# Banded attention beside a gated feed-forward layer: the second pass in blocks of 64 keys, its products with v in 64x32 tiles over two PSUM banks, and dense work in two banks

## The chip, the cores and the metric

The kernel runs on one core of one Trainium2 chip. The metric is device microseconds of one execution; the time before is the median of three runs, 883.07 us (882.6 to 883.37).

## The reference, cut to what matters

```python
xn = layernorm(x)                              # x: 2048 tokens x 512
q, k, v = split(xn @ wqkv)                     # 32 heads of 16
scores = q @ k.T * 16**-0.5                    # masked to 0 <= query - key < 256
s = (softmax(scores) @ v).reshape(...) @ wo
g = silu((silu(xn @ w1) * (xn @ w3)) @ w2)     # 512 -> 1792 -> 512
return x + s * g
```

Everything is float32. A query sees itself and the 255 keys before it.

## The kernel before, in words

**Tiling.** The 2048 tokens are cut in NT = 4 stretches t of TW = 512, the 32 heads in NG = 4 groups g of eight, and each group in two halves p of four heads. A unit is (t, g, p); there are 32. Dense products work on float32 numbers split in a high and a low float16 part, three products for one; a dense group is normally 12 matmuls of 128x128 by 512 columns into one PSUM bank: `project` (q or k, L423), `value` (v, L393), `gate_up` (w1 and w3, L684), `down` (w2, L729), `total` (wo, L771). `turn` (L355) transposes x on TensorE for a stretch; `powers` (L203) sums squares of weights in a tiny matmul. All of these, and the transposed maxima `pm` (L492), take their banks from the pool `psm` with three buffers of one bank.

**Attention in two passes.** The first pass (`pass1`) forms scores of 128 queries against up to 320 keys (L476) and takes each row's maximum on VectorE (L481). The maxima, in two float16 parts, become two more rows of q, so that the second pass gets score minus maximum straight from its matmul. The second pass (`pass2`) works with keys on the partitions: `scores(c)` writes a chunk of 128 keys by two blocks of 128 queries, for four heads, into a tile of two banks (L523; `s`, from the pool `pss`, two buffers of two banks, shared with the first pass). The mask is added on VectorE (L532 for a whole chunk, L537 for half of one), then ScalarE's exp (L541) writes `pt` in float32 into SBUF. `values(c)` multiplies `pt` by v (L551) in float32: for each head a tile of 128 rows by 32 columns of the array (16 of v, a column of ones for the sum, and columns that are not used), four heads beside each other, accumulated into `po` (pool `pso`, one bank). `finish` copies `po` out (L559). A unit of t > 0 has six chunks (CHUNKS), one of t = 0 has five (FIRST), the last of them half as wide.

**Order.** TensorE's order is that of the program. `batches` makes the rounds of a unit: in each, two of the second pass's score chunks or the first pass's row blocks (those of the unit two ahead) are emitted; in every second round the products with v that have been kept in `late` follow, and so do the transposed maxima. `spread` puts dense pieces between rounds, by cost. A dense group is two pieces of about six matmuls. The dense pieces of a unit come from two lists, `beside` (projections, v, output products) and the feed-forward's own, and are merged by position, so a group of one list can be half done while groups of the other pass. `later(n, f)` runs f after n more steps (a piece or a round is a step): the readers of a bank are partly emitted this way, one step late. Work marked `urgent` is put ahead on ScalarE's and VectorE's queues. After the last unit what remains of the feed-forward and the last output products run alone.

Of the kernel before, what the change touches and what calls it, by code (L numbers as in the profile page):

```python
# [2 lines left out]

# [17 lines left out]
P = 128  # L21
# [28 lines left out]
VB = 10  # L50
# [14 lines left out]
def tile_block(ctx: ExitStack, tc: tile.TileContext, x, wqkv, wo, w1, w3, w2, out):  # L65
# [18 lines left out]
    psm = pool("psm", 3, PSUM)  # L84
# [18 lines left out]


# [4 lines left out]
    def urgent():  # L109


        return tc.high_priority(offset=200) if started else nullcontext()
# [15 lines left out]
    def flush():  # L128
        while queue:
# [25 lines left out]
    M2 = const.tile([P, 2, P], BF16, name="M2")  # L155
    nc.vector.memset(M2, 0.0)
    nc.gpsimd.affine_select(M2[:, 0, :], M2[:, 0, :], pattern=[[-1, P]], base=0, channel_multiplier=1,
                            compare_op=ALU.is_gt, fill=NEG)
    nc.gpsimd.affine_select(M2[:, 1, :], M2[:, 1, :], pattern=[[1, P]], base=0, channel_multiplier=-1,
                            compare_op=ALU.is_ge, fill=NEG)  # L160
# [36 lines left out]
    def powers(sb, n, p2, inv):  # L197


        ps = psm.tile([P, n], F32, name="ps", tag="mm")  # L200
# [108 lines left out]
    def prepare(t):  # L309
# [32 lines left out]
        def turn(b):  # L342
# [5 lines left out]
            if t or b == 3:  # L348
                pt = psm.tile([P, NC, P], F32, name="mm", tag="mm")
            elif b == 2:  # L350
                pt = pso.tile([P, TW], F32, name="po").rearrange("p (k q) -> p k q", q=P)
            else:
                pt = pss.tile([P, 2, 512], F32, name="s")[:, 0, :].rearrange("p (k q) -> p k q", q=P)
# [25 lines left out]
    def value(j):  # L379
# [18 lines left out]
        return [(6, lambda h=h: part(h)) for h in range(2)]  # L398
# [8 lines left out]
    def project(t, g, k, terms=(range(3),)):  # L407
# [38 lines left out]
        return [(len(l), lambda n=n: part(n)) for n, l in enumerate(parts)]  # L446
# [59 lines left out]
    def pass2(t, g, p):  # L506
# [5 lines left out]

        def scores(c):
            qa, ka = QA[t, g], keys(t, g)
            n = sum(w for _, _, w in chunks[c]) * P
            s = pss.tile([P, 2, 512], F32, name="s")
            for a in range(2):
                o = 256 * a
                for j, q, w in chunks[c]:
                    for k in range(4):  # L520
                        r, h = k % 2, k // 2 * 64
                        rows = slice(64 * r, 64 * r + KR + 2)
                        nc.tensor.matmul(s[h:h + 64, r, o:o + w * P], ka[rows, 2 * p + a, (j + 2) * P + h:(j + 2) * P + h + 64],  # L523
                                         qa[rows, 2 * p + a, q * P:(q + w) * P], start=True, stop=True)
                    o += w * P

            sv = s.rearrange("p r (a b q) -> p (r a) b q", a=2, b=2)
            kinds = [{0: 1, 2: 0}.get(i - j) for j, q, w in chunks[c] for i in range(q, q + w)]
            if None not in kinds and len(kinds) == 2:
                m = M2 if kinds == [0, 1] else M2[:, kinds[0]:kinds[0] + 1, :].to_broadcast([P, 2, P])  # L530
                with urgent():
                    nc.vector.tensor_add(sv, sv, m.unsqueeze(1).to_broadcast([P, 4, 2, P]))  # L532
            else:
                for b, k in enumerate(kinds):
                    if k is not None:
                        with urgent():
                            nc.vector.tensor_add(sv[:, :, b, :], sv[:, :, b, :],  # L537
                                                 M2[:, k:k + 1, :].to_broadcast([P, 4, P]))
            cell[c] = pt = ppool.tile([P, 4, 256], F32, name="pt")
            with urgent():  # L540
                nc.scalar.activation(pt[:, :, 0:n], s.rearrange("p r (a q) -> p (r a) q", a=2)[:, :, 0:n], AF.Exp, scale=es)  # L541

        def values(c):
            if c == 0:
                cell["po"] = pso.tile([P, TW], F32, name="po")
            pt = cell.pop(c)
            o = 0
            for k, (j, q, w) in enumerate(chunks[c]):
                for i in range(4):
                    h = g * 8 + (i // 2) * 4 + 2 * p + i % 2  # L550
                    nc.tensor.matmul(cell["po"][32 * i:32 * i + 32, q * P:(q + w) * P],  # L551
                                     V[:, (4 * t + j) % VB, h * VW:h * VW + 32], pt[:, i, o:o + w * P],
                                     start=c == 0 and k == 0, stop=c == len(chunks) - 1, skip_group_check=True)
                o += w * P

        def finish():
            os = opool.tile([P, TW], F32, name="os")
            with urgent():
                nc.scalar.copy(os, cell["po"])  # L559
# [10 lines left out]
        def last():  # L570
            values(len(chunks) - 1)
            finish()
        n = len(chunks)
        return [lambda c=c: scores(c) for c in range(n)], [lambda c=c: values(c) for c in range(n - 1)] + [last]
# [98 lines left out]
    def gate_up(t, f):  # L673
# [38 lines left out]
        return [lambda k=k, half=half: part(k, half) for k in range(2) for half in range(2)]  # L712
# [368 lines left out]
```

## Time and profile before

| | |
|---|---|
| median of 3 runs | 883.07 us |
| the profiled execution: time, span | 881.5 us, 879.6 us |
| granted TensorE clock | 0.997 |
| busy: TensorE, VectorE, ScalarE, GpSimd | 846.5, 626.7, 443.1, 193.9 us |
| dense matmuls of 512 columns: gate and up (L684), down (L729), projections (L423) | 896 + 448, 672, 384 |
| scores of the second pass (L523), products with v (L551), instructions | 1920, 1920 |
| exp (L541) | 184 of 1093 ns, 200.9 us |

The lines are those of the kernel above. A call of a float32 matmul is two instructions on TensorE. A busy share is no rate: a matmul's duration holds its way through the array, and the next starts before it ends, so prices on TensorE are read from start to start. "Idle before" is the time in which an engine waited, and who ended it.

### The profile page before, as it was taken

What the parts mean: (1) busy time and instruction counts of PE and PEld (TensorE: products, weight loads), DVE (VectorE), ACT (ScalarE), POOL (GpSimd) and SP (SyncE); (2) the same over time, 40 slices, a digit from 0 to 9 for tenths busy, and PEclk for the clock granted to TensorE, in tenths of its full rate; (3) what the DMA queues carried; (4) which work ended last, traced back from release to release, by engine and by line L of the source; (5) the groups of instructions that cost most, each with busy time, mean ns of one, the idle gap of its engine ahead of it and who ended that gap; (6) DMA issues with size and microseconds to landing.
All of it is one profiled execution on the core that took longest, in us unless ns stands there. A gap on an engine that the chain in (4) does not pass through costs nothing.

```text
span 879.6 us, 20432 instructions
## 1 busy us (share of the span) xinstructions
PE 846.5 (96%) x7815; PEld 376.5 (43%) x7815; DVE 626.7 (71%) x1833; ACT 443.1 (50%) x650; POOL 193.9 (22%) x312
## 2 busy tenths in 40 slices
PE   9898898999999999999999999999999999999997
PEld 4333343444444444444444444444444444444443
DVE  8776876877778667787777775776767777666435
ACT  6975877473544444344444445443444444444421
POOL 2254245250201103121110111121111103131211
PEclk9999999999999999999999999999999999999999
DMA  9974534746433353353434344433442253332201
GB/s 293 253 244 148 151 110 126 236 132 222 128 108 70 93 155 107 104 143 98 134 104 103 93 109 135 140 85 104 115 124 84 81 134 115 106 104 82 78 10 59
DMA packets 95073, 110.43 MB, mean 126 GB/s; under 512 B 16960, under 2 KB 60288, under 8 KB 94976
## 3 DMA queue, kind: packets, MB, share of 16 engines
q1 hardware_dynamic: 94688, 108.62, 43.1%
q8 instruction: 61, 1.00, 0.5%
q10 hardware_dynamic: 288, 0.52, 0.2%
q14 instruction: 36, 0.29, 0.1%
HBM read 76.28 MB, written 28.57 MB: 119 GB/s over the span
## 4 chain that ended last, share of the span: by engine, by line
PE 70%; DVE 11%; ACT 5%; issue 4%; DMA 4%; POOL 3%; SPq 2%; POOLq 0%; DVEq 0%; ACTq 0%
PE mm L684 24%; PE mm L729 13%; PE po L551 8%; PE mm L423 6%; PE s L523 6%; PE mm L771 4%; PE s L476 4%; PE mm L393 3%; DVE junk L481 3%; POOL slot L224 2%; DVE s L532 2%; ACT pt L541 1%; DMA slot<-in_A_x_dram 1%; DMA slot<-in_B_w_dram 1%; SPq L590 1%
## 5 line engine op out<-in xcount | busy, mean ns | idle before, releaser
L541 ACT ACTIVATE pt<-s,es 128x1024 f32<-128x1024 f32 (+1 forms) x184 | 200.9, 1093 | 197.5 <-DVE s L532 101.0
L684 PE MATMUL mm<-XH,slot 128*128 128x512 f16 x896 | 268.1, 381 | 0.6 <-POOL slot L224 0.4
L224 POOL TENSOR_TENSOR slot<-slot,slot 128x256 f16<-128x256 f32 (+1 forms) x220 | 146.0, 689 | 529.2 <-ACT slot L708 401.2
L481 DVE CUSTOM_DVE_ANT_0 junk<-s,MW 128x320 bf16<-128x320 f32 x448 | 218.0, 487 | 27.3 <-PE s L476 16.2
L684 PEld LDWEIGHTS <-slot 128*128 128x128 f16 x1344 | 121.6, 98 | 158.9 <-issue 25.2
L684 PE MATMUL mm<-XL,slot 128*128 128x512 f16 x448 | 169.9, 379 | 0.0
L729 PE MATMUL mm<-slot,slot 128*128 128x512 f16 x672 | 160.1, 383 | 0.3
L537 DVE TENSOR_TENSOR s<-s,M 128x512 f32<-128x512 f32 x128 | 89.0, 696 | 62.2 <-PE s L523 53.9
L551 PE MATMUL po<-pt,V 128*32 128x128 f32 (+1 forms) x1920 | 98.3, 330 | 0.0
L729 PEld LDWEIGHTS <-slot 128*128 128x128 f16 x672 | 61.3, 98 | 80.6 <-issue 13.6
L476 PE MATMUL s<-KA,qa 48*64 48x320 f16 (+2 forms) x1024 | 73.6, 298 | 10.7 <-DVE M L481 5.2
L523 PE MATMUL s<-qa,KA 50*64 50x128 f16 (+1 forms) x1920 | 74.2, 251 | 9.9 <-ACT pt L541 6.6
L532 DVE TENSOR_TENSOR s<-s,M 128x1024 f32<-128x1024 f32 x56 | 68.7, 1227 | 15.3 <-PE s L523 13.2
L523 PEld LDWEIGHTS <-KA 50*64 50x64 f16 x1920 | 34.0, 105 | 85.1 <-issue 48.2
L708 ACT CAST slot<-slot 128x512 f16<-128x512 f32 x56 | 34.5, 616 | 61.7 <-DVE slot L704 61.6
L699 DVE SCALAR_TENSOR_TENSOR slot<-slot,mm 128x512 f32<-128x512 f32 x56 | 38.3, 684 | 35.2 <-ACT slot L695 35.1
L551 PEld LDWEIGHTS po<-pt,V 128*32 128x32 f32 x1920 | 49.8, 109 | 24.5 <-issue 11.3
L695 ACT ACTIVATE slot<-mm,sgs 128x512 f32<-128x512 f32 x56 | 38.2, 683 | 31.5 <-PE mm L684 29.8
L224 POOL TENSOR_TENSOR on<-on,rb 128x256 f32<-128x256 f32 x32 | 22.6, 727 | 130.3 <-DMA qa<-dm 50.4
L704 DVE SCALAR_TENSOR_TENSOR slot<-mm,slot 128x512 f32<-128x512 f32 x56 | 38.5, 688 | 17.7 <-PE mm L684 17.6
L745 DVE SCALAR_TENSOR_TENSOR slot<-mm,dsc,slot 128x512 f32<-128x512 f32 x48 | 35.9, 748 | 19.6 <-PE mm L729 19.4
L423 PE MATMUL mm<-XH,whi 128*128 128x512 f16 x128 | 47.2, 381 | 1.3 <-DVE slot L699 0.9
(128 smaller groups left out, 838.3 us busy)
## 6 DMA issues: line engine op xcount, KB each, us to landing
slot<-dW SPq DMA_DIRECT2D x126, 256.0 KB
slot<-in_B_w_dram SPq DMA_DIRECT2D x42, 256.0 KB
dW<-slot SPq DMA_DIRECT2D x42, 256.0 KB
slot<-in_A_x_dram SPq DMA_DIRECT2D x30, 256.0 KB
KA<-dK SPq DMA_DIRECT2D x24, 288.0 KB
qa<-dQ SPq DMA_DIRECT2D x32, 192.0 KB
dK<-slot SPq DMA_DIRECT2D x16, 256.0 KB
dQ<-slot SPq DMA_DIRECT2D x16, 256.0 KB
```

What stands on the lines that cost most here:

```text
L224: op(out[:, c], a[:, c], b[:, c])
L423: nc.tensor.matmul(cell["pp"], a[:, k, c, :], b[:, c, :], start=(c, i) == parts[0][0], stop=(c, i) == parts[-1][-1])
L476: nc.tensor.matmul(s[64 * c:64 * c + 64, r, :n], qa[rows, 2 * p + a, ii * P + 64 * c:ii * P + 64 * c + 64], ka[rows, 2 * p + a, e - n:e], ...
L481: nc.vector.tensor_tensor_reduce(out=junk[:, :n], in0=s[:, r, :n], in1=mask, scale=1.0, scalar=NEG, op0=ALU.add, op1=ALU.max, accum_out=M[ ...
L523: nc.tensor.matmul(s[h:h + 64, r, o:o + w * P], ka[rows, 2 * p + a, (j + 2) * P + h:(j + 2) * P + h + 64], qa[rows, 2 * p + a, q * P:(q + ...
L532: nc.vector.tensor_add(sv, sv, m.unsqueeze(1).to_broadcast([P, 4, 2, P]))
L537: nc.vector.tensor_add(sv[:, :, b, :], sv[:, :, b, :], M2[:, k:k + 1, :].to_broadcast([P, 4, P]))
L541: nc.scalar.activation(pt[:, :, 0:n], s.rearrange("p r (a q) -> p (r a) q", a=2)[:, :, 0:n], AF.Exp, scale=es)
L551: nc.tensor.matmul(cell["po"][32 * i:32 * i + 32, q * P:(q + w) * P], V[:, (4 * t + j) % VB, h * VW:h * VW + 32], pt[:, i, o:o + w * P], s ...
L684: nc.tensor.matmul(cell[k], w[:, (a * NC + c) * P:(a * NC + c + 1) * P], b[:, c, :], start=c == 0 and i == 0, stop=c == NC - 1 and i == 2)
L704: nc.vector.scalar_tensor_tensor(sg, cell[1], 0.5 * HS / (WS * XS)**2, sg, op0=ALU.mult, op1=ALU.mult)
L729: nc.tensor.matmul(ps, hh[:, a * TW + b * P:a * TW + (b + 1) * P], w[:, c * D:(c + 1) * D], start=f == f0 and i == 0, stop=f == f1 - 1 and ...
```

## The change

The second pass takes blocks of 64 keys. Even blocks lie in the lower 64 partitions, odd ones in the upper; a block is scored against the one to five blocks of 64 queries that see it. A piece is (block, first query block after it, how many, slot of 64 columns in the tile, whether v takes it). For t > 0 there are five chunks: two for each of the heads a = 0 and a = 1, and one for both; for t = 0 there are four. A chunk is still one exp of 128x1024. The masks are smaller and applied by slot, in up to two additions to a chunk.

Products with v run in tiles of 64 rows by 32 columns, the lower half of the partitions into the first bank of `po`, the upper half into the second; calls of two chunks alternate. `finish` copies the first bank on ScalarE and adds the second on VectorE. `pso` so has two banks and `psm` two instead of three. To work with two, the two pieces of a dense group are marked (`opening`) and kept next to each other in the list (`in_groups`, `more`); a round can still come between them. `powers` takes its bank from `pss` before the units start. A round with products with v counts 4 instead of 6 (COLS).

```diff
-COLS = 3
-CHUNKS = (((-2, 0, 1), (3, 3, 1)), ((-1, 0, 2),), ((0, 0, 2),), ((0, 2, 1), (1, 3, 1)), ((1, 1, 2),), ((2, 2, 2),))
-FIRST = (((0, 0, 2),), ((0, 2, 1), (1, 3, 1)), ((1, 1, 2),), ((2, 2, 2),), ((3, 3, 1),))
+COLS = 2
+AB = ((0,), (1,))
+CHUNKS = (*((a, ((0, 0, 5, 0, 1), (-2, 2, 3, 5, 1)), ((1, 0, 5, 0, 1), (5, 0, 3, 5, 1)),
+             ((0, 4, 2, 0, 0), (5, 2, 2, 1, 0))) for a in AB),
+          *((a, ((2, 0, 5, 0, 1), (6, 0, 2, 5, 1), (-4, 4, 1, 7, 1)), ((3, 0, 5, 0, 1), (7, 0, 1, 5, 1), (-3, 3, 2, 6, 1)),
+             ((0, 4, 2, 0, 0), (5, 2, 2, 0, 0))) for a in AB),
+          ((0, 1), ((4, 0, 4, 0, 1),), ((-1, 1, 4, 0, 1),), ((0, 3, 2, 2, 0),)))
+FIRST = (*((a, ((0, 0, 5, 0, 1), (6, 0, 2, 5, 1), (4, 3, 1, 7, 1)), ((1, 0, 5, 0, 1), (5, 0, 3, 5, 1)),
+            ((0, 4, 2, 0, 0), (5, 1, 1, 0, 0))) for a in AB),
+         *((a, ((2, 0, 5, 0, 1), (4, 0, 3, 5, 1)), ((3, 0, 5, 0, 1), (7, 0, 1, 5, 1), (3, 1, 2, 6, 0)),
+            ((0, 4, 2, 0, 0), (5, 1, 1, 0, 0))) for a in AB))
...
-    psm = pool("psm", 3, PSUM)
+    psm = pool("psm", 2, PSUM)
...
+    def opening(pieces):
+        for _, f in pieces[:-1]:
+            f.opens = True
+        return pieces
...
-    M2 = const.tile([P, 2, P], BF16, name="M2")
...
+    MK = const.tile([P, 3, 2, 64], BF16, name="MK")
...
-        ps = psm.tile([P, n], F32, name="ps", tag="mm")
+        ps = psm.tile([P, n], F32, name="ps", tag="mm") if started else pss.tile([P, 2, 512], F32, name="s")[:, 0, 0:n]
...
+        def pieces(c):
+            which, *halves, _ = chunks[c]
+            for n in range(max(map(len, halves))):
+                for a in which:
+                    for h in range(2):
+                        for piece in halves[h][n:n + 1]:
+                            yield 256 * a * (len(which) - 1) + 64 * piece[3], h, a, piece
...
+            for o, h, a, (m, k, n, _, _) in pieces(c):
+                for r in range(2):
+                    rows = slice(64 * r, 64 * r + KR + 2)
+                    nc.tensor.matmul(s[64 * h:64 * h + 64, r, o:o + 64 * n], ka[rows, 2 * p + a, 64 * (m + 4):64 * (m + 5)],
+                                     qa[rows, 2 * p + a, 64 * (m + k):64 * (m + k + n)], start=True, stop=True)
+            which, *_, masks = chunks[c]
+            sv = s.rearrange("p r (a k q) -> p (r a) k q", a=len(which), q=64)
+            for first, by, n, kind, of in masks:
+                v = sv[:, :, first:first + by * (n - 1) + 1:by, :]
+                with urgent():
+                    nc.vector.tensor_add(v, v, MK[:, kind, of:of + n, :].unsqueeze(1).to_broadcast([P, 2 * len(which), n, 64]))
...
+        def values(*cs):
+            if not begun:
+                cell["po"] = pso.tile([P, 2, TW], F32, name="po")
+            for group in zip_longest(*(pieces(c) for c in cs)):
+                for c, item in zip(cs, group):
+                    if item is None or not item[3][4]:
+                        continue
+                    o, h, a, (m, k, n, _, _) = item
+                    for r in range(2):
+                        i = 2 * r + a
+                        hd = g * 8 + r * 4 + 2 * p + a
+                        nc.tensor.matmul(cell["po"][32 * i:32 * i + 32, h, 64 * (m + k):64 * (m + k + n)],
+                                         V[64 * h:64 * h + 64, (4 * t + m // 2) % VB, hd * VW:hd * VW + 32],
+                                         cell[c][64 * h:64 * h + 64, r, o:o + 64 * n],
+                                         start=(h, i) not in begun, stop=c == len(chunks) - 1, skip_group_check=True)
+                        begun.add((h, i))
...
-                nc.scalar.copy(os, cell["po"])
+                nc.scalar.copy(os, po[:, 0, :])
+                c = slice(0 if t else 64, TW)
+                nc.vector.tensor_add(os[:, c], os[:, c], po[:, 1, c])
...
+        cols = [None, lambda: values(0, 1), None] + ([lambda: values(2, 3), lambda: last(4)] if t else [lambda: last(2, 3)])
...
+    def is_open(pieces):
+        return bool(pieces) and hasattr(pieces[-1][1], "opens")
+    def in_groups(pieces):
+        groups = []
+        for piece in pieces:
+            if groups and is_open(groups[-1]):
+                groups[-1].append(piece)
+            else:
+                groups.append([piece])
+        return groups
...
-        while ffn and (done[0] < want or ffn[0][0] == 0):
+        while ffn and (done[0] < want or ffn[0][0] == 0 or is_open(made)):
...
+    for i, k in enumerate((0, 2, 1)):
+        nc.sync.dma_start(MK[64:P, i], MK[0:64, k])
...
-        both = sorted([((i + 0.5) / len(l), k, i) for k, l in enumerate((beside[n], mine)) for i in range(len(l))])
-        spread(batches(u, units[n + 2] if n + 2 < len(units) else None), [(beside[n], mine)[k][i] for _, k, i in both])
+        lists = in_groups(beside[n]), in_groups(mine)
+        both = sorted([((i + 0.5) / len(l), k, i) for k, l in enumerate(lists) for i in range(len(l))])
+        spread(batches(u, units[n + 2] if n + 2 < len(units) else None), [piece for _, k, i in both for piece in lists[k][i]])
```

More of the change, by code (lines that the diff above doesn't have):

```diff
@@ L397, in part @@
                                          pv.rearrange("p (h d) -> p h d", d=DH), AF.Copy, scale=sc["uv"])
-        return [(6, lambda h=h: part(h)) for h in range(2)]
+        return opening([(6, lambda h=h: part(h)) for h in range(2)])
     QA = {}
@@ L568, in finish, with last @@
                 normalise(t, g)
-        def last():
-            values(len(chunks) - 1)
+        def last(*cs):
+            values(*cs)
             finish()
         n = len(chunks)
-        return [lambda c=c: scores(c) for c in range(n)], [lambda c=c: values(c) for c in range(n - 1)] + [last]
+        cols = [None, lambda: values(0, 1), None] + ([lambda: values(2, 3), lambda: last(4)] if t else [lambda: last(2, 3)])
+        return [lambda c=c: scores(c) for c in range(n)], cols
     def normalise(t, g):
@@ L711, in part @@
                 later(1, rest)
-        return [lambda k=k, half=half: part(k, half) for k in range(2) for half in range(2)]
+        return [q for k in range(2) for q in opening([(6, lambda k=k, half=half: part(k, half)) for half in range(2)])]
     ACC = {}
@@ L781, in part @@
                 give(y, XR[t, b])
-        return [(6, lambda h=h: part(h)) for h in range(2)]
+        return opening([(6, lambda h=h: part(h)) for h in range(2)])
     def total_by_columns(t, b):
```

58 lines of the change are left out of this document (14 added, 44 removed).

## The prediction

> **What bounds the kernel now.** I read the page first, for the engine that fills the span, then the timeline of TensorE, for what one round of attention costs between dense products, then the groups of instructions kept apart by shape, for the price of each edit, and the chain behind a dense bank on ScalarE and VectorE.
>
> The page (busy us, share of span, instructions; then TensorE and its granted clock in 40 slices):
>
> ```profile
> PE 846.5 (96%) x7815; PEld 376.5 (43%) x7815; DVE 626.7 (71%) x1833; ACT 443.1 (50%) x650; POOL 193.9 (22%) x312
> ...
> PE   9898898999999999999999999999999999999997
> ...
> PEclk9999999999999999999999999999999999999999
> ```
>
> TensorE is busy from end to end, at full clock. After 60 us the trace holds 2433 places where one 128x128 product of 512 columns follows another; they start 0.2165 us apart, and together these places lose only 2.8 us. So neither VectorE nor ScalarE sets the time: what takes TensorE time away counts, and so does what makes it wait.
>
> One stretch of it, by TensorE's timeline (start, duration, line; the start of the next row is the true price of a row, since durations overlap):
>
> ```profile
> 301.23 0.41 PE L523 MATMUL s<-qa,KA 50*64 50x256 f16 x8
> 301.47 0.31 PE L476 MATMUL s<-KA,qa 48*64 48x320 f16 x4
> 301.71 0.23 PE L492 MATMUL pm<-identh,nm 128*32 128x128 f16 x1
> 301.72 1.09 PE L551 MATMUL po<-pt,V 128*32 128x128 f32 x24
> 302.74 1.47 PE L729 MATMUL mm<-slot,slot 128*128 128x512 f16 x6
> 304.14 0.42 PE L523 MATMUL s<-qa,KA 50*64 50x128 f16 x16
> ```
>
> Scores of a chunk cost 0.24 us (L523 to L476), products with v of two chunks 1.02 us (L551 to L729). The six dense products before 304.14 take 1.30 us, and 0.1 to 0.16 more passes before scores begin. By the starts, over the whole trace, the 96 groups of L551 take 91.8 us and the 178 of L523 53 us.
>
> The shapes (busy, mean ns of one):
>
> ```profile
> L541 ACT ACTIVATE pt<-s,es 128x1024 f32<-128x1024 f32 x176 | 195.4, 1112 | 195.4 <-DVE s L532 101.0 <-DVE s L537 93.7
> L537 DVE TENSOR_TENSOR s<-s,M 128x512 f32<-128x512 f32 x128 | 89.0, 696 | 62.2 <-PE s L523 53.9 <-PE s L476 6.6 <-ACT O L595 1.5
> L532 DVE TENSOR_TENSOR s<-s,M 128x1024 f32<-128x1024 f32 x56 | 68.7, 1227 | 15.3 <-PE s L523 13.2 <-PE s L476 2.0
> L551 PEld LDWEIGHTS po<-pt,V 128*32 128x32 f32 x1920 | 49.8, 109 | 24.5 <-issue 11.3
> ```
>
> And what holds a dense bank after its last product (ScalarE's tanh, then VectorE's product, of a gate whose last matmul began at 507.18):
>
> ```profile
> 507.18 0.38 PE L684 MATMUL mm<-XL,slot 128*128 128x512 f16 x1
> ...
> 507.59 0.69 ACT L695 ACTIVATE slot<-mm,sgs 128x512 f32<-128x512 f32 x1 [0.20 <-PE mm L684]
> ...
> 508.56 0.68 DVE L699 SCALAR_TENSOR_TENSOR slot<-slot,mm 128x512 f32<-128x512 f32 x1
> ```
>
> That bank is free at 509.24, 1.84 us after its products (507.18 + 0.22). Over the 56 gates the median is 1.9; six of the first 14 take 2.8 to 5.3. For up (L704) and down (L745) it is about 1.0.
>
> **The change part by part.**
>
> *Products with v (L551).* A group is priced by the columns that one column tile streams. Sixteen instructions with 512 columns to a tile take 1.004 us (32 groups), eight with 128 take 0.358 (8 groups): 1.68 ns a column and 0.143 us for entering and leaving. The 24-instruction groups (512 columns too, in shorter calls) take 1.015. A unit (t, g, p) of t>0 now has three such groups, 1.015 + 1.015 + 1.004 = 3.03 us; one of t=0 has 1.015 + 1.004 + 0.358 = 2.38. After it, 64 keys and 32 output columns fill an eighth of the array, and both halves of the partitions go at once into two banks. Counted from the new CHUNKS, a tile streams 8 slots of 64 = 512 columns in values(0,1), 512 in values(2,3) and 256 in last(4): 1.004 + 1.004 + 0.574 = 2.58, if eight tiles run side by side as four do. FIRST has twice 512: 2.01. The trace has four column tiles at once (L551) and two by two at once (L523, rows and columns), but no eight; the bounds are this and no overlap of the two halves at all (below). I take the lower end, since L523 overlaps across rows at full rate, and add 0.15 and 0.09 a unit: pieces of 64 columns stream in 54 ns but their weights load in 109, and eight tiles start later than four. So 2.73 and 2.10: 24 x 0.30 + 8 x 0.28 = 9.4 us less.
>
> The Trainium skill, in "TensorE: Matmul & The Clock Gate" (Measured speedup vs the span model), gives 16 tiles 10.6 times one, 0.66 of the ideal. Applied to what would remain to be streamed (24 x 1280 and 8 x 1024 columns at 1.68 ns, 65 us), this would make 98 us of the 91.8, 6.5 more instead of 9.4 less. No row here has more than four tiles at once, so the trace can't show it.
>
> *Scores (L523).* Chunks go from 6 to 5 for t>0 and from 5 to 4 for t=0, each still 512 columns to a tile. That removes 24 x 0.245 and 8 x 0.14 (the half chunk) = 7.0 us; the pieces of 64 columns in two chunks of each t>0 unit put back some 0.03 each, 1.4. Net 5.6 less.
>
> *Rounds* (the code's batches). For t>0 the order stays at seven (the last one or two hold rows of the first pass alone). For t=0 it is six instead of seven: one switch from dense work to scores (0.156 us, 177 times in the trace) and part of one back, 0.2 x 8 = 1.6 us less.
>
> *Exp and masks.* Exps go from 184 to 152, 201 to 169 us on ScalarE; masks go from 157.7 us to 123 by a line through the two rows (165 ns + 1.04 ns an element: 430 ns for 256, 298 for 128, 696 for 512; 4.14 us a unit of t>0, 2.9 of t=0), and each unit adds one VectorE addition of 512 elements for the second bank (0.69, 22 us in all), after ScalarE's copy. All lie beside TensorE; a chunk's way to its exp is 0.86 us of masks instead of 0.70 or 1.23. So zero, within 3 us either way: if scores waited that 0.16 us more in all 120 chunks of t>0, not hidden by the next round (3 us later), it would be 19, but the trace's waits of scores on exp are only eight (6.6 us). The output bank pair is held 0.7 us longer at the end of a unit; its next writer comes at least two rounds later, some 6 us, so nothing.
>
> *Dense work with two banks instead of three.* This is the price. Each dense group is 12 products, 2.6 us, so a bank freed within 2.6 us of its last product costs nothing when groups are whole and alternate. Most are, by the rows above. The exceptions: the long releases of the first 14 gates, which exceed 2.6 by 6.6 us in all, of which rounds of attention in between cover about half, so 3; and other tenants. The 12 sets of transposes of t>0 (L355) take 0.5 us and hold their bank through a cast and a subtraction (0.58 + 0.69 and starts, about 1.9); between two halves of a group (1.3 us) that leaves 0.6 for the next, 12 x 0.5 = 6. The transposed maxima (pm, 31 of them) are copied in 0.25 us and followed by 1 us of products with v: nothing. Sum 9, between 3 and 32: the upper end has half of these 51 places (pm, transposes, 8 sums for scales) wait out a whole release of 1.25 us.
>
> The Trainium skill says the same against the change in "TensorEngine Tiling (Array Packing)" (Restrictions and Gotchas): row tiles must write different banks, which raises PSUM pressure.
>
> *Start.* Three short mask DMAs stand on SP's queue ahead of the first weight loads (rows of 0.4 us there), 1 us in a phase where the DMA engines are full anyway; the first projections lack a third bank, about 1 us. I put 1.5; 0 to 3.
>
> **Sum.** 9.4 + 5.6 + 1.6 - 9 - 1.5 = 6.1 us less. The profiled execution took 881.5 (span 879.6 and 1.9 around it), so 875.4; the median of the runs is 1.6 higher, so 877.
>
> **The rivals.**
>
> *Two banks hold dense work up (slower).* Place: the first product of a group on L684, L423 or L393. It decides once banks cost more than 15 us, what attention saves after the start. At 32 us the time is 900; I take 893 as typical. For: in the trace two groups are open side by side, and the third bank is in use. Against: with one group half done, the others already alternate between two banks, and dense products still lose only 2.8 us. 20%.
>
> *The halves don't stream side by side (slower).* Columns to a tile double: 1.865 + 1.865 + 1.004 = 4.73 instead of 3.03, +1.70 x 24, and 1.865 + 1.65 instead of 2.38, +1.14 x 8: 50 us more in place of 9.4 less, so 877 + 59 = 936; a quarter of that loss gives 892. It decides from some 6 us of loss on. For it: no row has eight tiles. Against it: L523, whose two row halves pass 512 columns a tile in 0.24 us, four tiles at once. 13%. The Trainium skill's ratio above would come out near the quarter, at 893.
>
> *Two banks cost nothing,* and scores wait less as ScalarE has 32 us less: 877 - 11 = 866. For: releases of 1.0 to 1.9 under 2.6. 12%.
>
> **Numbers.** My forecast, 877, has 55%, by its bounds 866 to 884. A measurement tells 0.2% (1.8 us) from no change. Faster: 0.48 of the forecast's 0.55 and 0.12, so 0.60; same 0.04 of it; slower 0.03 and 0.20 and 0.13, so 0.36. The range from 864 to 900 leaves out the full loss of overlap and the worst of the banks.
>
> **What would show it.** Products with v at about 1.0, 1.1 and 0.6 us a group and some 82 us together, 152 exps, scores at some 47 us, dense products with some 10 us of waits ahead of their first of 12, mostly near transposes and before 160 us. A group of products with v near 1.9 us, or waits of TensorE on L699, L704 or L363 beyond 15 us, would make it wrong.

## The result and the profile after

The changed kernel takes 890.92 us, the median of eight runs (886.62 to 895.13), beside 883.23 for the kernel before on the same chip (882.59 to 884.02): 1.0093 times as long, 95% interval 1.0066 to 1.0121. By the medians that is 7.7 us slower; 6 us less were forecast. The profiled execution took 886.6 us with a span of 884.4, against 881.5 and 879.6 before: it is the fastest of the eight, so its stretches below account for 4.8 us of the 7.7.

The page of the changed kernel (busy us, share, instructions; TensorE in 40 slices; its granted clock):

```profile
PE 839.2 (95%) x8327; PEld 370.2 (42%) x8327; DVE 602.3 (68%) x1961; ACT 415.4 (47%) x618; POOL 196.4 (22%) x314
...
PE   7898868999999999999999999999999999999997
...
PEclk9999999999999999999999999999999999999999
```

Every engine but GpSimd has less to do, and the time is longer. Forty slices are too coarse to show where. The same two stretches of 40 us on both kernels do show it (stretch, its length, then busy us and instructions of TensorE, its weight loads, VectorE, ScalarE, GpSimd, the granted clock, DMA share, GB/s). Before:

```profile
90.00:130.00 40.00, 38.94 (x322) 16.84 (x322) 31.11 (x116) 30.22 (x53) 14.67 (x23) 0.96 0.45 133
130.00:170.00 40.00, 36.35 (x340) 16.65 (x333) 30.18 (x100) 26.82 (x49) 17.90 (x28) 1.00 0.63 187
```

After:

```profile
90.00:130.00 40.00, 32.03 (x276) 13.86 (x276) 27.63 (x106) 26.28 (x48) 14.22 (x22) 0.96 0.44 137
130.00:170.00 40.00, 32.40 (x282) 14.52 (x280) 22.48 (x82) 22.63 (x40) 14.62 (x24) 0.87 0.52 159
```

TensorE, VectorE and ScalarE all do less in the same time: they wait for one another. These are the units of t = 0, where weights are still prepared. From 60 us to the end of unit 8, by TensorE's starts, the changed kernel needs 241.7 us against 232.2, so it loses 9.5. In units 9 to 31 (t > 0) it needs 548.5 against 553.3, so it gains 4.8, as forecast in kind.

The parts that the change made do what it says. One stretch of TensorE's timeline at t > 0 (start, duration, line; L547 scores, L495 rows of the first pass, L511 transposed maxima, L573 products with v, L757 down):

```profile
310.69 0.42 PE L547 MATMUL s<-qa,KA 50*64 50x320 f16 x12
310.94 0.31 PE L495 MATMUL s<-KA,qa 48*64 48x320 f16 x4
311.18 0.23 PE L511 MATMUL pm<-identh,nm 128*32 128x128 f16 x1
311.33 1.09 PE L573 MATMUL po<-pt,V 64*32 64x320 f32 x32
312.36 1.47 PE L757 MATMUL mm<-slot,slot 128*128 128x512 f16 x6
```

Thirty-two instructions in eight tiles, with 512 columns to a tile, pass in 1.03 us (311.33 to 312.36): the two halves of the partitions stream side by side. One row is dearer than it was: the products with v now begin 0.15 us after the transposed maxima (311.18 to 311.33). Before, it was 0.01 (301.71 to 301.72).

Groups of the changed kernel, apart by shape (busy, mean ns | idle before):

```profile
L557 ACT ACTIVATE pt<-s,es 128x1024 f32<-128x1024 f32 x152 | 168.9, 1114 | 181.3 <-DVE s L554 175.9
L554 DVE TENSOR_TENSOR s<-s,MK 128x256 f32<-128x256 f32 x224 | 95.0, 427 | 56.4 <-PE s L547 50.6 <-PE s L495 5.2
L573 PEld LDWEIGHTS po<-pt,V 64*32 64x32 f32 x2880 | 43.8, 106 | 28.0 <-issue 7.2
```

There are 152 exps and 168.9 us of them, and a mask of 256 elements takes 427 ns, both as worked out beforehand.

**How a bank is held up.** TensorE's timeline of the changed kernel in t = 0 (in brackets: idle before, and who ended it; L442 a projection, L712 gate and up, L374 the transposes):

```profile
121.63 0.38 PE L442 MATMUL mm<-XL,whi 128*128 128x512 f16 x1
...
125.49 0.38 PE L712 MATMUL mm<-XL,slot 128*128 128x512 f16 x1
128.94 0.59 PE L712 MATMUL mm<-XH,slot 128*128 128x512 f16 x2 [3.07 <-DVE slot L455]
...
132.79 1.11 PE L374 MATMUL mm<-identf,slot 128*128 128x128 f32 x4 [2.31 <-DVE slot L727]
...
134.52 1.04 PE L712 MATMUL mm<-XH,slot 128*128 128x512 f16 x2
135.34 0.63 PE L712 MATMUL mm<-XL,slot 128*128 128x512 f16 x1
135.77 0.63 PE L712 MATMUL mm<-XH,slot 128*128 128x512 f16 x1
```

Two waits of 3.07 and 2.31 us, ended by VectorE's readers of a projection (L455) and of a gate (L727). VectorE had itself been waiting for ScalarE:

```profile
128.19 0.69 DVE L455 SCALAR_TENSOR_TENSOR slot<-mm,slot 128x512 f16<-128x512 f32 x1 [2.44 <-ACT slot L451]
...
132.05 0.69 DVE L727 SCALAR_TENSOR_TENSOR slot<-slot,mm 128x512 f32<-128x512 f32 x1 [1.97 <-ACT slot L723]
```

And ScalarE's own readers of the same two banks stand behind a cast of weights (L247) that waits for GpSimd, which makes low parts (L243) from 125 to 134 us without a break:

```profile
126.31 0.62 ACT L247 CAST slot<-slot 128x512 f16<-128x512 f32 x1 [1.07 <-POOL slot L243]
127.56 0.60 ACT L451 ACTIVATE slot<-mm 128x512 f16<-128x512 f32 x1 [0.64 <-POOL slot L243]
...
131.33 0.69 ACT L723 ACTIVATE slot<-mm,sgs 128x512 f32<-128x512 f32 x1 [0.64 <-POOL slot L243]
```

```profile
125.15 8.74 POOL L243 TENSOR_TENSOR slot<-slot,slot 128x256 f16<-128x256 f32 x13
```

So the bank was full and its products done, but the copy that has to come before it is freed had its turn only after work of another kind. The Trainium skill, in "TensorE: Matmul & The Clock Gate" (Architectural detail), says that ScalarE and VectorE are strictly first in, first out. These rows agree with it: the projection's last product starts at 121.63, and L451, which copies its bank, at 127.56.

The rows hold a second reason. L451 and L723 themselves wait their last 0.64 us for GpSimd. By the kernel, what they wait for can only be the `slot` that they write: slots come from one shared pool in SBUF (`take`, `give`), and GpSimd is not done with what the slot held before. The cast L247 waits for the same kind of thing. Which part of the delay is the place in the queue and which the late slot is not parted by any run.

The kernel before has such a delay too, without a wait. There a projection's last product starts at 146.42 and its bank is free at 151.44, 4.8 us after its products:

```profile
146.42 0.38 PE L423 MATMUL mm<-XL,whi 128*128 128x512 f16 x1
...
150.14 0.57 ACT L432 ACTIVATE slot<-mm 128x512 f16<-128x512 f32 x1
...
150.75 0.69 DVE L436 SCALAR_TENSOR_TENSOR slot<-mm,slot 128x512 f16<-128x512 f32 x1 [2.60 <-ACT slot L432]
```

No wait of TensorE in that trace ends with L436; there two more banks were left to go on with. In the changed kernel the bank of 121.63 is free at 128.88, 7.0 us after its products, and TensorE stands.

The granted clock shows in the last rows of TensorE: after the second wait products of 512 columns start 0.41 to 0.43 us apart (134.52, two of them, 135.34, 135.77) where the usual distance is 0.2165.

### The profile page after: what moved, and what is told of

Same layout as the page of the kernel before. It is cut to its first block, busy times and chain, and to the rows that moved or that the text cites. A ratio compares the mean times of both kernels' runs of the same rounds, so it can differ in the third digit from the quotient of the medians.

```text
span 884.4 us, 21601 instructions
## 1 busy us (share of the span) xinstructions
PE 839.2 (95%) x8327; PEld 370.2 (42%) x8327; DVE 602.3 (68%) x1961; ACT 415.4 (47%) x618; POOL 196.4 (22%) x314
## 4 chain that ended last, share of the span: by engine, by line
PE 66%; DVE 12%; ACT 7%; issue 6%; POOL 4%; DMA 4%; SPq 1%; POOLq 0%; ACTq 0%; DVEq 0%
PE mm L712 24%; PE mm L757 14%; PE po L573 7%; PE mm L442 6%; PE s L547 4%; POOL slot L243 4%; PE s L495 4%; PE mm L799 3%; PE mm L412 3%; DVE junk L500 3%; ACT pt L557 2%; DVE s L554 2%; DMA slot<-in_B_w_dram 1%; DVE slot L732 1%; DMA dr<-dd 1%
## 5 line engine op out<-in xcount | busy, mean ns | idle before, releaser
L712 PE MATMUL mm<-XH,slot 128*128 128x512 f16 x896 | 269.7, 383 | 8.6 <-DVE slot L455 4.0
L243 POOL TENSOR_TENSOR slot<-slot,slot 128x256 f16<-128x256 f32 (+1 forms) x220 | 147.4, 696 | 499.9 <-ACT slot L736 350.3
L557 ACT ACTIVATE pt<-s,es 128x1024 f32<-128x1024 f32 x152 | 168.9, 1114 | 181.3 <-DVE s L554 175.9
L500 DVE CUSTOM_DVE_ANT_0 junk<-s,MW 128x320 bf16<-128x320 f32 x448 | 217.8, 486 | 43.6 <-PE s L495 33.7
L712 PEld LDWEIGHTS <-slot 128*128 128x128 f16 x1344 | 123.4, 98 | 167.0 <-issue 29.0
L554 DVE TENSOR_TENSOR s<-s,MK 128x256 f32<-128x256 f32 (+2 forms) x280 | 121.1, 435 | 76.7 <-PE s L547 70.8
L712 PE MATMUL mm<-XL,slot 128*128 128x512 f16 x448 | 170.8, 381 | 0.0
L757 PE MATMUL mm<-slot,slot 128*128 128x512 f16 x672 | 157.6, 382 | 0.6 <-DVE XL L382 0.2
L757 PEld LDWEIGHTS <-slot 128*128 128x128 f16 x672 | 61.9, 98 | 80.8 <-issue 12.1
L573 PE MATMUL po<-pt,V 64*32 64x320 f32 (+4 forms) x2880 | 89.7, 347 | 0.0
L495 PE MATMUL s<-KA,qa 48*64 48x320 f16 (+2 forms) x1024 | 72.8, 299 | 12.2 <-DVE M L500 6.2
L547 PE MATMUL s<-qa,KA 50*64 50x320 f16 (+3 forms) x1472 | 62.5, 261 | 4.3 <-DVE M L500 3.3
L723 ACT ACTIVATE slot<-mm,sgs 128x512 f32<-128x512 f32 x56 | 38.4, 685 | 47.1 <-PE mm L712 44.3
L547 PEld LDWEIGHTS <-KA 50*64 50x64 f16 x1472 | 31.4, 105 | 68.4 <-issue 34.4
L243 POOL TENSOR_TENSOR on<-on,rb 128x256 f32<-128x256 f32 x32 | 23.1, 744 | 163.0 <-DMA qa<-dm 98.3
L727 DVE SCALAR_TENSOR_TENSOR slot<-slot,mm 128x512 f32<-128x512 f32 x56 | 38.4, 686 | 28.9 <-ACT slot L723 28.9
L732 DVE SCALAR_TENSOR_TENSOR slot<-mm,slot 128x512 f32<-128x512 f32 x56 | 38.5, 688 | 25.9 <-PE mm L712 25.3
L573 PEld LDWEIGHTS po<-pt,V 64*32 64x32 f32 x2880 | 43.8, 106 | 28.0 <-issue 7.2
L442 PE MATMUL mm<-XH,whi 128*128 128x512 f16 x128 | 47.3, 381 | 4.7 <-DVE slot L455 1.6
L495 PEld LDWEIGHTS <-qa 48*64 48x64 f16 x1024 | 29.9, 106 | 45.2 <-issue 23.9
```

Of the source, the lines that this page charges most:

```text
L243: op(out[:, c], a[:, c], b[:, c])
L442: nc.tensor.matmul(cell["pp"], a[:, k, c, :], b[:, c, :], start=(c, i) == parts[0][0], stop=(c, i) == parts[-1][-1])
L495: nc.tensor.matmul(s[64 * c:64 * c + 64, r, :n], qa[rows, 2 * p + a, ii * P + 64 * c:ii * P + 64 * c + 64], ka[rows, 2 * p + a, e - n:e], ...
L500: nc.vector.tensor_tensor_reduce(out=junk[:, :n], in0=s[:, r, :n], in1=mask, scale=1.0, scalar=NEG, op0=ALU.add, op1=ALU.max, accum_out=M[ ...
L547: nc.tensor.matmul(s[64 * h:64 * h + 64, r, o:o + 64 * n], ka[rows, 2 * p + a, 64 * (m + 4):64 * (m + 5)], qa[rows, 2 * p + a, 64 * (m + k ...
L554: nc.vector.tensor_add(v, v, MK[:, kind, of:of + n, :].unsqueeze(1).to_broadcast([P, 2 * len(which), n, 64]))
```

## Experiments

Times are medians; each ratio is to the kernel before on the same chip, with its 95% interval, and need not be exactly that of the medians. In the diffs, "whole groups" means the hunks `opening`, `is_open`, `in_groups` and the lists of units, as in the change.

**One part of the change at a time.** The first kernel is the one before with the change's order of dense work only (three banks, old second pass); the second has the two banks as well, and one PSUM bank lies unused.

```diff
# both: the kernel before with whole groups
+        lists = in_groups(beside[n]), in_groups(mine)
# the two-bank kernel in addition
-    psm = pool("psm", 3, PSUM)
+    psm = pool("psm", 2, PSUM)
-        ps = psm.tile([P, n], F32, name="ps", tag="mm")
+        ps = psm.tile([P, n], F32, name="ps", tag="mm") if started else pss.tile([P, 2, 512], F32, name="s")[:, 0, 0:n]
```

> The kernel before with whole dense groups and still three dense banks. Theory A: within 3 us of before, 880 to 886, since no bank is short. Theory B: the same. Theory C, the order of whole groups costs: as slow as its two-bank sister, over 890.

> The kernel before with its old second pass, but dense groups whole and psm with two banks (one PSUM bank is left unused). Theory A, two banks cost: in the changed kernel TensorE waited some 20 us ahead of dense products for banks whose readers (L451, L723) stand on ScalarE behind casts of weights that wait for GpSimd; the same must show here without any of the new attention work, 12 to 25 us slower than before (895 to 908 us), with most of it between 90 and 170 us. Theory B, the new second pass itself shifts the work of t=0 so that dense products come too early: here within 3 us of before. Theory C, whole groups instead of interleaved halves cost: as slow as the kernel with whole groups and three banks, run beside it.

Whole groups alone: 890.03 us, 1.0066 (1.0042 to 1.009), 6 us slower. Two banks on top: 905.01 us, 1.0242 (1.0216 to 1.0268), another 15. Against the latter the changed kernel (1.0093) is 13 us faster, and that is the worth of the new second pass. So +6 + 15 - 13 = +8, which is the change; the 13 is what is left between two runs, measured with two banks only.

What TensorE waited for from 60 to 300 us (waiting line, who ended it: us in total, times, longest). With whole groups and three banks:

```profile
PE s L482 <- DVE M L487: 6.7, 4, 4.2
PE mm L690 <- DVE slot L442: 2.3, 1, 2.3
...
PE mm L361 <- DVE XL L369: 0.8, 1, 0.8
```

With two banks:

```profile
PE mm L361 <- DVE slot L442: 7.0, 2, 4.1
PE s L482 <- DVE M L487: 6.8, 4, 3.9
PE mm L690 <- DVE XL L369: 2.1, 1, 2.1
PE mm L690 <- DVE slot L710: 1.2, 1, 1.2
```

Two waits of the transposes (L361) on a projection's readers (L442) make up half of the difference of the two kernels up to unit 8: 250.8 us against 236.8, so 14.0. Over the whole span, readers of projections (L442) end 13.2 us of TensorE's waits with two banks and 2.3 with three, 10.9 more, where the kernel is 15 slower. In units 9 to 31 the two kernels need 558.3 and 558.0: with the old second pass a third dense bank is worth nothing there.

**Three banks only where they matter.** The changed kernel with the old second pass and a third dense bank at t = 0, and its own second pass with 2 + 2 banks from unit 8 on (groups whole throughout; VectorE's scratch for squares has one buffer instead of two).

```diff
+    psx = pool("psx", 1, PSUM)
+    def dense(shape, dtype, name="mm"):
+        turns[0] += 1
+        if third[0] and turns[0] % 3 == 0:
+            return psx.tile(shape, dtype, name=name, tag="x")
+        return psm.tile(shape, dtype, name=name, tag="mm")
-        rows2, cols2 = pass2(*u) if u else ([], [])
+        rows2, cols2 = (pass2 if u[0] else pass2_first)(*u) if u else ([], [])
+        if n == 8:
+            third[0] = False
```

> The changed kernel, but the units of t=0 use the second pass of before (one output bank) and leave the other output bank to dense work as a third one; from t=1 on two output banks and two dense banks as changed. Theory A with its waits mostly in t=0: the loss of the stretch 90 to 170 us goes and the gain of t=1 to 3 stays, so 875 to 880. Theory B: also faster, by the old second pass in t=0, but then the two-bank kernel with the old second pass is no slower than before. If instead the waits of t=1 to 3 are what costs: 886 or more.

883.27 us, 0.9995 (0.9979 to 1.0012): the time of the kernel before. The loss of 8 is gone once t = 0 has its old second pass and three banks, although groups stay whole there. It was expected to be faster than before, 875 to 880. A further step keeps the interleaved half groups up to unit 7 as well and picks the third bank from a list of those that are free:

```diff
+        tag = next(b for b in idle if third[0] or b != "x")
+            if whole_now[0] and groups and is_open(groups[-1]):
```

> In t=0 the second pass of before, three dense banks and halves interleaved as before; whole groups from the seventh unit on, and from t=1 the changed second pass with two output and two dense banks. By the study so far (whole groups alone cost 6 us, most of it in t=0; the loss of the changed kernel comes before 175 us): t=0 costs nothing against before, and t=1 to 3 gain what the changed kernel gained there, 3 to 5 us, so 878 to 881. If whole groups or two banks cost as much in t=1 to 3 as the new pass saves: 883 to 886.

882.62 us, 0.9991 (0.9973 to 1.0009), no better, where 878 to 881 were expected. Its units 9 to 31 take 549.5 us, 3.8 less than before, and all of it is given back up to unit 8 (236.0 against 232.2).

**The other tenants moved out of the two banks.** Here transposes of t > 0 and the sums for scales take a tile of the scores.

```diff
-            if t or b == 3:
+            if t == 0 and b == 3:
```

> The changed kernel, with the transposes of t=1 to 3 and all sums of weights in the score banks instead of the two dense banks; the transposed maxima stay. My prediction put 6 us on the transposes. Theory A as predicted, small tenants are what waits: 5 to 8 us faster than the changed kernel, 883 to 886. Theory A with long releases in t=0 as the cause: under 3 us faster, since the banks are held by projections and gates there. Worse than the changed kernel by over 3 us: score banks are the scarcer ones.

901.64 us, 1.0216 (1.0182 to 1.025), 11 us worse than the change. TensorE's waits over the whole span show the new ones (L222 the weight sums, L374 the transposes, now in `s`):

```profile
PE s L222 <- DVE M L500: 5.1, 4, 2.2
...
PE s L374 <- DVE M L500: 3.6, 2, 2.1
```

Both wait for a tile whose rows VectorE (L500) has not yet reduced: a tile of the scores is scarcer than a dense bank. Since this put a new wait in the place of the old one, it says nothing of what those tenants cost in the two banks.

**Is it GpSimd's queue?** The low parts of w3 are moved from GpSimd to VectorE, in the kernel before, in the changed one, and in the mixed one.

```diff
-                    split_pool(a[k][:, 0:D], a[k][:, D:], raws[i][k], pi[:, k, i:i + 1])
+                    (split if k else split_pool)(a[k][:, 0:D], a[k][:, D:], raws[i][k], pi[:, k, i:i + 1])
```

> The kernel before with the same shift of w3's low parts to VectorE. Both theories: three banks ride over the delay, so within 3 us of before, 880 to 886. Over 4 us faster would mean that the first stretch is held by GpSimd with three banks too, and that the shift's gain in the changed kernel says little of banks.

> The changed kernel; the low parts of w3 in t=0 are made by VectorE (one ScalarE cast with scale and one VectorE operation for two ScalarE operations and two GpSimd halves), which takes 14 x 1.3 = 18 us off GpSimd and 14 x 0.7 = 10 us off ScalarE. Theory A1, in t=0 the two banks are held because their readers stand on ScalarE behind weight casts that wait for GpSimd: the waits of 2 to 3 us near 125 and 130 us go, 8 to 14 us faster than the changed kernel, 877 to 883. Theory A2, two banks are short whatever holds them: under 3 us faster, 888 or more.

> The mixed kernel with w3's low parts on VectorE. If the shift is worth nothing with three banks and interleaved halves: as the mixed kernel within 2 us. If GpSimd's backlog bounds t=0 there too: 3 to 6 us faster than the mixed kernel.

Before: 877.21 us, 0.9922 (0.9907 to 0.9938), 7 us faster. Changed: 889.6 us, 1.0062 (1.0041 to 1.0083), within reach of the change itself. Mixed: 876.74 us, 0.9909 (0.9887 to 0.9931). So with three banks less work on GpSimd's queue pays, and with two it doesn't, although GpSimd had been named at the end of each chain above. For the kernel before, both theories had expected no gain. To take it further, GpSimd's subtractions were left out for w1 and w3, then for w2 as well, so that this queue has little left that could be late:

```diff
# all three weights; for w1 and w3 alone the same line, switched on at their call
-        halves(nc.gpsimd.tensor_sub, lo, raw, hi)
+        nc.gpsimd.memset(lo, 0.0)
```

> The kernel before with the same left out. By the shift of w3 to VectorE, which gave this kernel 7 us, it should gain 6 to 10 us, 874 to 878. Theory A1: the changed kernel gains more than this one by 4 us or more, since here a third bank rides over a part of the delay. Theory A2: both gain the same.

> The changed kernel, leaving out the low parts of w1 and w3 (GpSimd sets them to zero, 28 memsets for 56 subtractions of 0.69 us, some 35 us less on GpSimd; nothing is added to VectorE or ScalarE). Theory A1, two banks are costly in t=0 because their readers stand on ScalarE behind casts that wait for GpSimd: 10 to 16 us faster than the changed kernel, 875 to 881. Theory A2, banks are short in t=0 whatever GpSimd does: not more than 5 us faster, 886 or more.

> The kernel before with the same left out. Both theories: 7 to 10 us faster, 873 to 877, as when w1's and w3's were left out. The difference between this and the changed kernel with the same left out is what the change costs without GpSimd's backlog: under 4 us by A1, 10 or more by A2.

> The changed kernel, leaving out the low parts of all three weights of the feed-forward (one GpSimd memset in place of two subtractions, 42 times). Theory A1, readers of the two banks stand on ScalarE behind casts that wait for GpSimd: with no backlog left the waits of TensorE for L727 and L455 before 300 us fall below 3 us in all, and the kernel is at least 12 us faster than the changed one, 876 to 880. Theory A2, two banks are too few: 884 to 890.

> The old second pass with whole groups and two dense banks, and the same left out. A1: the 21 us that this kernel lost against before shrink to 6 to 9 (whole groups alone cost 6): 880 to 885. A2: it still loses 15 or more against the kernel before with the same left out: 890 or more.

| low parts left out | before | changed | before, whole groups, two banks |
|---|---|---|---|
| none | 1 | 1.0093 (1.0066 to 1.0121) | 1.0242 (1.0216 to 1.0268) |
| w1, w3 | 0.993 (0.9907 to 0.9953) | 1.0104 (1.0067 to 1.0141) | |
| w1, w3, w2 | 0.9894 (0.9871 to 0.9917) | 1.001 (0.9997 to 1.0024) | 1.0125 (1.0105 to 1.0146) |

In the last row the changed kernel takes 884.94 us and the one before 874.39: the gap is 10.5 us where it was 7.7, and the two-bank kernel's is 20.4 where it was 21.0. So GpSimd's backlog makes all three slow, but it is not what whole groups and two banks cost. Of the two theories in the expectations, A1 (the readers stand behind GpSimd's backlog) fell, and A2 (two banks are too few, whatever holds them) stood, except that it let both kernels gain alike from w1 and w3. What ends the waits then is seen in the changed kernel without low parts (TensorE, then ScalarE, then VectorE):

```profile
149.61 0.38 PE L442 MATMUL mm<-XL,whi 128*128 128x512 f16 x1
149.82 1.46 PE L757 MATMUL mm<-slot,slot 128*128 128x512 f16 x6
155.50 1.09 PE L374 MATMUL mm<-identf,slot 128*128 128x128 f32 x4 [4.21 <-DVE slot L455]
```

```profile
150.80 0.63 ACT L197 ACTIVATE sqa<-slot 128x512 bf16<-128x512 f32 x1 [1.76 <-DMA slot<-in_B_w_dram]
...
152.65 0.57 ACT L451 ACTIVATE slot<-mm 128x512 f16<-128x512 f32 x1
```

```profile
152.01 0.69 DVE L199 CUSTOM_DVE_ANT_0 sqd<-slot 128x512 bf16<-128x512 f32 x1 [3.27 <-DMA slot<-in_B_w_dram]
...
154.75 0.69 DVE L455 SCALAR_TENSOR_TENSOR slot<-mm,slot 128x512 f16<-128x512 f32 x1
```

The projection's last product began at 149.61, and its copy could have started then. ScalarE and VectorE stood at squares of weights (L197, L199) whose DMA had not landed; behind them come L451 at 152.65, then first-pass maxima, and L455 at 154.75. The transposes wait 4.21 us. It is the same chain with a DMA in GpSimd's place: a reader of a bank queued behind weight preparation that is not ready. This part is read from one trace; no run took the DMA's wait alone away.

Last, in the kernel before, the low parts of w2 computed on VectorE as well as those of w3 (w1's stay on GpSimd):

```diff
# beside the edit for w3 above
-            split_pool(b[:, 0:D], b[:, D:], raw2, sw[:, f - f0:f - f0 + 1])
+            split(b[:, 0:D], b[:, D:], raw2, sw[:, f - f0:f - f0 + 1])
```

> The kernel before, nothing left out, with the low parts of w3 and of w2 made by VectorE. w3's alone gave 7 us. If GpSimd's backlog is what held t=0: 7 to 10 us faster than before, 874 to 877. If VectorE has become the limit there: less than w3's alone, over 878.

878.81 us, 0.9943 (0.9926 to 0.9959): no better than w3 alone.

**The 0.15 us after the transposed maxima.** They are made 128 columns wide, like the dense products, and put first in their round, so that no product with v follows them (the lines that change the order are left out here).

```diff
-            pm = psm.tile([32, P], F16, name="pm", tag="mm")
+            pm = psm.tile([P, P], F16, name="pm", tag="mm")
...
-                nc.scalar.copy(mt, pm)
+                nc.scalar.copy(mt, pm[0:32])
```

> The changed kernel; the transposed maxima (L511) go ahead of a round's scores, right behind dense work, and as a full 128x128 tile (the maxima padded with zeros to 128 columns), so that TensorE has no other tile shape in between. In the changed kernel the maxima (128x32) pass 0.15 us before the products with v (64x32), in the kernel before 0.01 us. Theory, each change of tile shape costs 0.15 us: 32 x 0.14 = 4 us faster than the changed kernel, 886 to 888. Rival, the 0.15 us is a wait for something else (weights of the first product with v): the gap moves to the next row and nothing is gained, 889 to 892.

> The mixed kernel with w3 on VectorE, and the maxima first in the round as a full tile. In t=1 to 3 the changed shape costs 3.3 us there: 873 to 875 if the shape is the cause, 876 to 878 if not. In t=0, where maxima and products with v had the same shape before, nothing or 1 us lost.

Changed: 890.94 us, 1.0095 (1.0067 to 1.0123), no difference. Mixed, with w3 on VectorE: 878.87 us, 0.9958 (0.9941 to 0.9976), 2 us worse than without, where a gain of 2 or no change was expected. TensorE's timeline of the first of the two (L515 maxima, L551 scores, L499 rows, L577 products with v):

```profile
313.59 0.22 PE L515 MATMUL pm<-identh,nm 128*128 128x128 f16 x1
313.74 0.42 PE L551 MATMUL s<-qa,KA 50*64 50x320 f16 x12
313.98 0.31 PE L499 MATMUL s<-KA,qa 48*64 48x320 f16 x4
314.22 1.09 PE L577 MATMUL po<-pt,V 64*32 64x320 f32 x32
```

The 0.15 us has moved: it now passes from the maxima to the scores (313.59 to 313.74). From the last dense product to the scores it is then 0.37 us (0.2165 and 0.15) where it was 0.31, so the maxima themselves cost less than the 0.15 of before. But in units 9 to 31 the scores' share by starts grows from 34.9 to 37.3 us, in part by longer waits of the rows for ScalarE's exp (4.0 to 6.1 us). The time is the one that the expectation's rival gave, so that the tile's shape is what makes the 0.15 us rests on the traces of the two kernels and is not shown by these runs.

## Why the prediction was wrong

It came out as the first rival, "Two banks hold dense work up", which had 20% and was priced at 893 with 900 at its worst. The number is near in part by luck: 6 us of the loss come from whole groups, which that rival does not name. The changed kernel by the prediction's steps:

- **What bounds the kernel** held: TensorE's time sets the end, and in units 9 to 31 less work on it gave 4.8 us.
- **Products with v** held. Eight tiles stream side by side: 1.03 us for each group of 512 columns to a tile, 1.19 for those of values(2,3) with their smaller pieces, 0.595 for last(4), so 2.81 a unit of t > 0 where 2.73 was worked out. By starts 91.8 became 84.3, 7.5 less instead of 9.4. The second rival (no overlap, or a quarter less) fell, and with it the prediction's use here of the ratio for 16 tiles that it took from the Trainium skill's page "TensorE: Matmul & The Clock Gate" (Measured speedup vs the span model): 98 us by that estimate, 84.3 measured with eight tiles.
- **Scores and rounds** held roughly: scores 53.1 to 48.7 us, 4.4 less instead of 5.6. From dense products to scores, rows or transposes 33.6 became 31.0 us (27.6 + 5.8 + 0.2 to 18.1 + 8.6 + 4.3), 2.6 less, where 1.6 was worked out for the rounds. These sums hold waits; without them they are 21.5 and 20.5, 1.0 less.
- **Transposed maxima**: put at nothing; 0.5 became 5.1 us. That is 0.14 to 0.15 us each time, where the tile's shape now goes from 128x32 to 64x32. Before, both had 128x32, and no row of that trace passed from the one shape to the other.
- **Order of dense work**, that is whole groups, had no term at all, and this is a step that failed: the prediction took it for what makes two banks bearable. It costs 6 us by itself (890.03 against 883.98 beside it). In the prediction's own words, two groups open side by side used the third bank; what that bought was not asked.
- **Two banks**: 9 us with bounds 3 and 32; 15 measured (905.01 - 890.03), inside the bounds but mis-sized, and put on the wrong bank. Six of the nine were to come from the 12 sets of transposes of t > 0, whose bank the next group would wait for, and three from the long releases of the first 14 gates. The place was partly right: from 60 us on the six waits of over 1 us for a dense bank lie before 165 us, and three of them stand at transposes. But there it is the transposes that wait, for the bank of a projection, a gate or a weight sum. The other step that failed is the release time of a bank: gates, ups and downs were priced from their readers (1.0 to 1.9 us in the median), projections were not priced at all. With three banks such a release was already 4.8 us at 146.42 and cost nothing; with two it was 7.0 (121.63), and the wait of one group delays the readers of the next. In the changed kernel the readers of projections (L455) end 8.8 us of TensorE's waits over the whole span, none before. Those of gates, ups and transposes (L727, L732, L382) end 8.1 us, so the prediction's own sign, over 15 us of these, did not appear.
- **Start**: 1.5 us were set, 0 to 3. The first scores of the second pass start at 67.68 us instead of 66.94, 0.7 later, and 86 dense products have started by 40 us instead of 96.

The miss by steps: 6.0 for whole groups, 4.5 for the banks with the start (15 against 9 + 1.5), 3.3 for the second pass (16.6 forecast, 13.3 between the two runs; the maxima take 4.6 of it). That is 13.8, from the forecast of -6.1 to the measured +7.7. It comes out even because the 13.3 is what the other two leave.

**What stays open.** Why whole groups cost 6 us with three banks isn't shown. In the profiled executions the span is 9.3 us longer (888.9 against 879.6): 4.6 by unit 8, with four waits of rows on VectorE's maxima (6.7 us in the list above, 1.9 before), and 4.7 in units 9 to 31, where the trace shows one wait of 2.0 us and a lower clock after it. Whether two banks would do if projections gave theirs back sooner, by more SBUF slots or by their readers further ahead in the queues, was not run. The kernels with three banks at t = 0, whole groups (883.27) and interleaved ones (882.62), can't be told apart.

**A version faster than both** came out on the way: the kernel before with w3's low parts on VectorE, 877.21 us, 0.9922 (0.9907 to 0.9938). With the new second pass from t = 1 on it is 876.74, 0.9909 (0.9887 to 0.9931); the intervals overlap, so the second pass adds nothing that these runs can tell.

## What to carry to other kernels

In this case a PSUM bank was worth what its slowest releases cost, not their median, and the slowest belonged to a tenant that nobody had priced. List every kind of work that takes the bank, and for each ask what else stands in the in-order queues of the engines that read it, and what that work waits for. Where a change takes a buffer away and rearranges work to do without it, the rearrangement has a price of its own, and the stage with the worst queues decides for both. When every engine is less busy and the time is longer, compare the same stretch of both traces: the loss lies where all of them do less at once.

## What the runs showed of the hardware

- Eight tiles of 64x32 run as fast side by side as four of 128x32: 1.03 us for 512 columns to a tile in float32, against 1.00; with smaller pieces 1.19.
- From the transposed maxima to the products with v it is 0.15 us on TensorE where the tile's shape changes between them, 0.01 where it doesn't. The Trainium skill, in "TensorEngine Tiling (Array Packing)" (Key Properties), says that changing the tiling mode drains the engine; these two traces agree with it.
- Where TensorE has waited, its next products of 512 columns can start 0.43 us apart instead of 0.2165, for some 3 us: after one wait of 2.18 us (before, from 90.3), of 2.03 (whole groups, from 791), after 3.07 and 2.31 (changed, from 134.5), but also after waits of 0.92 and 0.85 (changed, from 157.4), and not after one of 1.63 (before, at 153.5). In the changed kernel 20 such distances cost 4.1 us, in the one before 8 cost 1.5. The granted clock of the stretch from 130 to 170 us is 0.87 where it was 1.00, 0.96 with whole groups alone and 0.83 with two banks (stretches of those two below). A wait on a bank can thus cost more than its own length.

```profile
130.00:170.00 40.00, 37.16 (x311) 16.89 (x310) 30.75 (x96) 28.21 (x49) 20.86 (x32) 0.96 0.60 181
```

```profile
130.00:170.00 40.00, 29.79 (x224) 12.78 (x222) 20.56 (x65) 24.58 (x44) 19.21 (x30) 0.83 0.52 159
```
